# Masks from GpSimd, the up-projection weights in halves, and a new order of the instructions in an attention and maxout kernel

## The chip, the cores and the metric

The kernel runs on one core of a Trainium2 chip. A core has five engines that run side by side, each with its own queue of instructions in a fixed order, and that wait for each other only by semaphores: TensorE (PE, matmuls and transposes; its weight loads are listed as PEld), VectorE (DVE), ScalarE (ACT), GpSimd (POOL) and SyncE (SP), which here only issues DMAs. DMAs move data between the main memory (HBM) and the on-chip buffer (SBUF); matmuls write into eight banks of PSUM, from which DVE or ACT copy. The metric is the device time of one execution in microseconds (us), smaller is better.

## What is computed

Four batches of attention with 8 heads, 768 positions and 64 elements per head, then a feed-forward layer over all 3,072 tokens.

```python
scores = scale * np.matmul(q, k.transpose(0, 1, 3, 2))
stream_keep = causal & (is_sink | in_win)
mask = np.where(retr[0, :, 0, 0, None, None], full_mask, stream_mask)
scores = np.where(mask[None, :, :, :], scores, -1000000000.0)
scores = scores - np.max(scores, axis=-1, keepdims=True)
a = np.exp(scores)
a = a / (np.sum(a, axis=-1, keepdims=True) + 1e-09)
attn = np.matmul(a, v)
x = np.ascontiguousarray(attn_out.transpose(0, 2, 1, 3)).reshape(B * S, H * D)
out = np.maximum(x @ w1, x @ w2) @ w_out      # 512 -> 1024 -> 512
```

Three of the eight heads (`is_retrieval`) are causal over all earlier positions; the other five see the first 4 positions (sinks) and a window of 64.

## The kernel before, in words

**Heads and tiles.** The kernel finds at run time which heads are full and sorts the heads (`head_order`, L1483), so that four pairs of heads are worked: full with full, full with streaming, and two pairs of streaming heads (`SLOTS`). Each batch is worked in two halves of 384 queries, written (b, hf). Of the scores only blocks of 128 keys by 128 queries that some mask lets through are computed; the tables `GROUP0` (first halves), `GROUP1` (second halves) and `GROUP_A` (first half of batch 0) put these blocks into score tiles of two PSUM banks each. For streaming heads a "mixed" key block holds the 64 sink positions beside 64 positions of the window (`mix_k`, `mix_v`, tiles `kx`, `vx`).

**Steps of one half.** q, k and v arrive as float32 in a slot of `ld` (three slots, which the two up-projection weights share with the batches). They are cast to bf16 (`cast_qk` into `qb`, `cast_v` into `vb`), q and k are turned by PE (`turn`, L712, into a PSUM bank) and copied out (`unturn`, into `qk`). Score tiles (L893, 64 rows of the array at a time, two heads beside each other) are exponentiated by ACT from PSUM into `at` (L912, six buffers), masked by DVE through a product with 0/1 masks (L931), and multiplied with v (`weighted`, L956), where a column of ones gives the sum. DVE divides (L973, L983) into `x`. `x` is turned by PE in batch 0 (L1086) and by a DMA in the others (L1105). In (0, 0) the masks are added to the scores by matmuls of the identity with rows of the mask table instead (L867). For batch 3, q, k and v are cast by the DMA that loads them (`load_pair`, L558, issued by POOL) and turned by DMA (L583).

**Feed-forward.** max(h1, h2) = relu(h1 - h2) + h2, so the kernel prepares w12 = w1 - w2 (four subtractions on DVE, L1122, a quarter of the columns each) and w2·w_out (`prep_weights`: cast w2 to `w2b`, turn it, L1138, and multiply it by `wob`, the bf16 w_out, L1156). For each half, `forward` does 32 up-projection matmuls (L1177) with relu on ACT or DVE (L1201, L1203), and 12 matmuls per 128 tokens (L1227): four of x with w2·w_out and eight of the relu with w_out. The result goes over `ot` to HBM (L1246).

**What sets the order.** Nothing here is scheduled by the compiler. The program records operations with their costs, dependencies, PSUM claims and ranks (`Op`, `Order`), and `Order.run` (L190) plays them against a model of the engines, the PSUM banks and the DMA rings. In the order in which that play begins them, they are emitted into the engines' queues. For PE it takes the first list in `PE_LISTS` whose next operation is ready for at least a `MARGIN`; for DVE, ACT and POOL, an operation that several could do goes to the one that would be done first, waiting operations in order of `RANK`. While nothing is ready before 38 us of that model, PE gets dummy matmuls on a tile of zeros (L471), which keep its clock up. Parameters such as `RANK`, `MARGIN`, `LOADS`, `RATE`, `STEP` were found by a search over orders.

**Loads.** `LOADS` gives the first loads in order: A and B are q and k of the first and second half of batch 0, Av and Bv their v, w10 to w23 the quarters of w1 and w2, wo0 to wo3 the quarters of w_out. SP issues them (`whole` L513, `piece` L523 for v, `load_up` L608), w_out goes through POOL with a cast (L616). The mask table, 128 x 1,152 in bf16, is a constant in HBM: its first 128 columns (the identity) are loaded from ACT's queue (L1570), the other 1,024 from SP's (L595) behind q and k. From it DVE makes 0/1 masks (`kept`, L646).

**Runs of scores.** `TOGETHER` (L113) names which score tiles are issued as one operation of PE: in pairs for all halves but the first, where they are single.

## Time and profile before

| | |
|---|---|
| time, median of 3 runs | 184.38 us (184.33 to 184.59) |
| the profiled execution's own time | 183.78 us |
| its span, first to last instruction | 180.9 us |
| granted TensorE clock | 0.999 |
| PE busy | 171.1 us (95%) |
| ACT busy | 131.7 us (73%) |
| DVE busy | 96.7 us (53%) |
| POOL busy | 42.8 us (24%) |
| DMA | 32.67 MB, mean 181 GB/s |

The profile is one execution, taken by the hardware. Line numbers (L1177) are those of the kernel before; a helper that records operations of many kinds has one line for all (L480 is every copy on ACT, L482 every copy on DVE or POOL). The rows are of these kinds: busy time of each engine in a stretch (us of the span, with the number of instructions, the granted clock PEclk as a share, the busy share of the DMA engines and GB/s); the chain that ended last (start, length, what, xN instructions merged); the timeline (start, length, engine, line, operation, out<-in, shape, count, and in brackets how long the engine had been idle and what ended that); groups by line. A busy PE is not PE at its peak, because the ends of pipelined matmuls are modelled.

### The profile page before, as it was taken

What the parts mean: (1) busy time and instruction counts of PE and PEld (TensorE: products, weight loads), DVE (VectorE), ACT (ScalarE), POOL (GpSimd) and SP (SyncE); (2) the same over time, 40 slices, a digit from 0 to 9 for tenths busy, and PEclk for the clock granted to TensorE, in tenths of its full rate; (3) what the DMA queues carried; (4) which work ended last, traced back from release to release, by engine and by line L of the source; (5) the groups of instructions that cost most, each with busy time, mean ns of one, the idle gap of its engine ahead of it and who ended that gap; (6) DMA issues with size and microseconds to landing.
All of it is one profiled execution on the core that took longest, in us unless ns stands there. A gap on an engine that the chain in (4) does not pass through costs nothing.

```text
span 180.9 us, 4911 instructions
## 1 busy us (share of the span) xinstructions
PE 171.1 (95%) x1816; PEld 106.2 (59%) x1836; DVE 96.7 (53%) x283; ACT 131.7 (73%) x287; POOL 42.8 (24%) x77
## 2 busy tenths in 40 slices
PE   7899599989999999999999999999999999999992
PEld 7767486466747656565545565565466645545561
DVE  3456796599788985576247476656448500000000
ACT  3399695597999999999996984677798524525421
POOL 0000710100609488799671000000000000000000
PEclk9999999999999999999999999999999999999999
DMA  5999999999999999999999999160151052012013
GB/s 139 323 253 336 343 224 242 344 298 278 254 297 273 323 293 284 150 250 217 147 102 136 236 173 200 66 145 0 62 145 62 0 145 116 11 58 116 0 60 125
DMA packets 74929, 32.67 MB, mean 181 GB/s; under 512 B 54162, under 2 KB 71826, under 8 KB 74898
## 3 DMA queue, kind: packets, MB, share of 16 engines
q1 hardware_dynamic: 54704, 28.71, 64.9%
q0 software_dynamic: 19904, 3.41, 26.4%
q8 instruction: 16, 0.26, 0.6%
q10 hardware_dynamic: 290, 0.16, 0.3%
q14 instruction: 15, 0.12, 0.2%
HBM read 25.46 MB, written 6.29 MB: 176 GB/s over the span
## 4 chain that ended last, share of the span: by engine, by line
PE 73%; SPq 11%; DMA 6%; ACT 3%; DVE 3%; issue 2%; DVEq 0%; ACTq 0%
PE ps L1227 32%; PE ps L1177 24%; PE ps L893 7%; PE ps L956 7%; DMA ld<-in_v_dram 6%; SPq L523 5%; SPq L608 4%; PE ps L712 3%; ACT at L912 2%; SPq L513 2%; DVE w L1122 1%; SPq L595 1%; ACT qk L480 1%; DVE vx L482 1%; DVE vb L482 0%
## 5 line engine op out<-in xcount | busy, mean ns | idle before, releaser
L912 ACT ACTIVATE at<-ps 128x512 bf16<-128x512 f32 (+2 forms) x134 | 64.9, 595 | 3.5 <-PE ps L893 1.9
L1177 PE MATMUL ps<-xt,w 128*128 128x384 bf16 x256 | 46.0, 326 | 0.9 <-DVE w L1122 0.6
L1227 PE MATMUL ps<-wob,g 128*128 128x512 bf16 (+1 forms) x192 | 45.3, 370 | 0.4
L1177 PEld LDWEIGHTS <-w 128*128 128x128 bf16 x256 | 23.5, 98 | 15.9 <-issue 0.9
L1201 ACT ACTIVATE g<-ps 128x384 bf16<-128x384 f32 x56 | 27.5, 503 | 7.0 <-PE ps L1177 6.5
L931 DVE TENSOR_TENSOR at<-at,tab 128x1024 bf16<-128x1024 bf16 (+5 forms) x49 | 25.5, 537 | 12.7 <-ACT at L912 12.4
L1227 PEld LDWEIGHTS <-g 128*128 128x128 bf16 x200 | 18.1, 98 | 17.6 <-issue 0.2
L480 ACT COPY ot<-ps 128x512 f32<-128x512 f32 (+1 forms) x20 | 11.4, 572 | 22.8 <-PE ps L1227 22.7
L1227 PE MATMUL ps<-w2o,xt 128*128 128x512 bf16 (+1 forms) x91 | 24.2, 370 | 0.6
L956 PEld LDWEIGHTS <-at 128*128 128x128 bf16 x477 | 19.8, 97 | 7.3 <-issue 0.2
L983 DVE TENSOR_TENSOR x<-ps,rez 128x192 f32 x64 | 22.8, 356 | 1.8 <-DVE x L983 0.2
L956 PE MATMUL ps<-vb,at 128*128 128x65 bf16 x387 | 21.6, 193 | 0.0
L893 PE MATMUL ps<-qk 64*128 64x128 bf16 (+1 forms) x322 | 20.1, 230 | 0.3
L482 POOL CAST qb<-ld 128x384 bf16 x23 | 11.9, 551 | 35.5 <-DMA ld<-in_k_dram 35.5
L893 PEld LDWEIGHTS <-qk 64*128 64x128 bf16 x322 | 11.9, 94 | 11.2 <-issue 8.2
L1227 PEld LDWEIGHTS <-xt 128*128 128x128 bf16 x100 | 9.2, 98 | 8.8 <-issue 0.2
L480 ACT COPY qk<-ps 128x768 bf16<-128x768 bf16 x17 | 12.9, 817 | 0.6 <-PE ps L712 0.6
L471 PE MATMUL ps<-warmer 128*128 128x128 bf16 x147 | 12.1, 250 | 1.1 <-POOL warmer L1564 1.1
L712 PE MATMUL ps<-tab,qb 128*128 128x128 bf16 x144 | 10.4, 219 | 2.9 <-POOL qb L482 2.1
L480 ACT CAST qb<-ld 128x384 bf16 (+1 forms) x23 | 8.8, 452 | 5.1 <-DMA ld<-in_k_dram 3.1
L471 PEld LDWEIGHTS <-warmer 128*128 128x128 bf16 x147 | 10.9, 115 | 1.4 <-POOL warmer L1564 1.1
L712 PEld LDWEIGHTS <-qb 128*128 128x128 bf16 x144 | 8.4, 98 | 4.0 <-POOL qb L482 2.7
(62 smaller groups left out, 146.1 us busy)
## 6 DMA issues: line engine op xcount, KB each, us to landing
out_dram<-ot SPq DMA_DIRECT2D x23, 256.0 KB, 2.3
ld<-in_q_dram SPq DMA_DIRECT2D x6, 768.0 KB, 6.8
ld<-in_k_dram SPq DMA_DIRECT2D x6, 768.0 KB, 7.7
ld<-in_v_dram SPq DMA_DIRECT2D x18, 256.0 KB, 6.7
ld<-in_moe_w_dram SPq DMA_DIRECT2D x8, 512.0 KB, 8.2
wob<-in_moe_w_out_dram POOLq DMA_DIRECT2D x4, 256.0 KB, 8.5
ld<-in_q_dram POOLq DMA_DIRECT2D x8, 96.0 KB, 7.0
ld<-in_k_dram POOLq DMA_DIRECT2D x8, 96.0 KB, 7.2
```

The source lines that it names most:

```text
L471: nc.tensor.matmul(banks[e][:, 0:128], lhsT=warm, rhs=warm, start=True, stop=True)
L480: nc.scalar.copy(out=out, in_=in_)
L482: eng[e].tensor_copy(out=out, in_=in_)
L712: nc.tensor.transpose(to[:, i], qbs[:, T["qb", n, hf] % NQB, t, i].rearrange("p h d -> p (h d)"), ident)
L893: nc.tensor.matmul(to.rearrange("p (i c) -> p i c", c=128), lhsT=lhsT, rhs=q_of(n, i, m)[rows], start=bk not in under, stop=True, skip_gro ...
L912: nc.scalar.activation(out=at[:, bk, 0:w], in_=bank(("ps", b, hf, t), part=bk)[:, 0:w], func=ACT.Exp, scale=scale,)
L931: eng[e].tensor_tensor(out=at, in0=at, in1=tbl, op=ALU.mult)
L956: nc.tensor.matmul(po[:, hh, i - NT * hf, :], lhsT=ats[:, T["at", b, hf, t] % NAT, bk, e * 128:(e + 1) * 128], rhs=rhs, start=first, stop= ...
L983: nc.vector.tensor_tensor(out=xs[:, (2 * b + hf) % NX, :, bass.ds(heads[2 * p + hh], 1), :], in0=po[:, hh, :, 0:D].unsqueeze(2), in1=z[:, ...
L1177: nc.tensor.matmul(bank(key)[:, 0:HALF], lhsT=w[:, kc, fc * 128:(fc + 1) * 128], rhs=xts[:, (2 * b + hf) % NXT, :, kc, :], start=(kc == 0) ...
L1201: nc.scalar.activation(out=g, in_=ph, func=ACT.Relu)
L1227: nc.tensor.matmul(bank(key)[:, cols], lhsT=lhsT, rhs=(w2o if kind == "x" else wob)[:, c, cols], start=(e == 0), stop=(e == len(steps) - 1),)
```

## The change

Before and after compute the same. Six things differ.

1. **Masks.** The constant in HBM and its two loads are gone. DVE zeroes the table and POOL fills it: `affine_select` once for the identity and seven times in `mask_table` for the additive masks, and two copies. The order's model takes the masks as given at 6.5 us.
2. **w1 and w2 in two parts of columns.** Each is loaded in two pieces of 512 columns instead of four of 256. The four subtractions and casts stay quarters, each waiting for the half that it lies in.
3. **q and k of batch 0 apart.** `SPLIT` now holds (0, 1) beside (0, 0). q and k of these halves are cast by separate operations (those of (0, 0) were before), and new for both: turned by separate PE operations (`TQ` for q, `TK` for k) into banks of their own, and copied out by separate copies.
4. **Scores in runs.** `TOGETHER` is gone, every score tile is an operation of its own. The order prefers a further score tile when the last PE operation was one, starts a run only when `S_RUN` tiles are ready with banks free (`run_of_scores`), and its model counts a price for entering and leaving a run.
5. **Loads of w_out** are held back by POOL: each but the first copies one element of an earlier load's place (`landed`) before it issues, and so waits for that load. The model limits outstanding descriptors on POOL's ring too.
6. **The order searched anew**: all ranks, margins and rates, with ranks of their own for batch 0 (`FRONT`, `rank_of`), eight `at` buffers instead of six, and a new `LOADS`. The buffer of the final test on the sums (`ok`) now lies in a load slot.

The general path for other head patterns (`tile_any_heads`), which doesn't run here, uses three score matmuls of 256 columns instead of two of 384.

```diff
--- before
+++ after
...
-TOGETHER = (
-    [[0, 1], [2, 3], [4, 5], [6]], [[0, 1], [2, 3], [4, 5], [6, 7], [8, 9]],
-    [[0], [1], [2], [3], [4], [5]],
-)
...
+    def run_of_scores(self, first, t):
+
+        mine = self.lists["S"][first:]
+        mine = [o for o in mine if o.tag[1:3] == mine[0].tag[1:3]]
+        n = 1 if self.stuck or mine[0].tag[1:3] == (0, 0) else min(S_RUN, len(mine))
+        if len(mine) - n == 1 and not self.stuck:
+            n += S_REST
+        if any(o.left or o.ready > t + 1e-9 for o in mine[:n]):
+            return False
+        return sum(e is None for e in self.banks) >= 2 * n
...
-                    for n in names:
+                    for n in ("S", *names) if last == "S" else names:
...
+                        if n == "S" and last != "S" and not self.run_of_scores(at[n], t):
+                            continue
...
+                        extra = ENTER_S if n == "S" and last != "S" else LEAVE_S if last == "S" and n != "S" else 0.0
+                        last = n
...
+MASKS_MADE = 6.5
...
-NAT = 6
+NAT = 8
...
-PE_LISTS = ('TX', 'W', 'S', 'TQ', 'P', 'H', 'P2', 'F')
-PLACES = (0, 1, 2, 0, 1, 2, 0, 1, 2, 0, 1, 2)
+PE_LISTS = ('TX', 'W', 'S', 'TK', 'TQ', 'P', 'H', 'P2', 'F')
...
-LOADS = (
-    'A', 'Av', 'B', 'w23', 'wo0', 'wo1', 'wo2', 'w20', 'wo3', 'w21', 'w11', 'w10', 'w12', 'w22',
-    'w13', 'Bv',
-)
-BIAS = {'DVE': 1, 'ACT': 0}
+LOADS = ('A', 'wo0', 'B', 'w20', 'w10', 'Av', 'wo1', 'wo2', 'w11', 'wo3', 'w21', 'Bv')
+BIAS = {'DVE': 0, 'ACT': 0}
...
-PACE = 0
+PACE = 1
...
-SPLIT = ((0, 0),)
+RING = {'SP': 4224, 'POOL': 6200, 'ACT': 4224}
+SPLIT = ((0, 0), (0, 1))
...
+S_RUN = 2
+S_REST = 1
+ENTER_S = 0.1
+LEAVE_S = 0.11
...
-MARGIN = {'W': 2.0, 'S': 0.8, 'F': 2.0, 'TQ': 0.8}
-X_MARGIN = 1.5
+MARGIN = {'W': 1.2, 'S': 0.3, 'F': 0.3, 'TQ': 1.2}
+X_MARGIN = 0.8
...
+FRONT = (
+    {'mix_k': -14.4, 'mask': -3.2, 'unturn': 13.5, 'exp': 11.7, 'vcast': 31.8, 'cast': -27.9,
+    'norm': -5.0}, {'vcast': 9.0, 'unturn': -0.2, 'exp': 16.7, 'mask': 0.7, 'norm': -5.5,
+    'mix_k': 13.8, 'cast': -1.4},
+)
+FRONT_STEP = (22.5, 5.2)
+UNTURN_BIAS = ({'ACT': 1.0}, {})
+SHARED = 0.89
+UP_PARTS = 2
...
+    def rank_of(kind, b, hf, at=0):
+        if b:
+            return RANK[kind]
+        return RANK[kind] + FRONT[hf].get(kind, 0.0) + FRONT_STEP[hf] * at
...
-    def load_table(lo, hi):
-        return dma(0.262, lambda _: nc.sync.dma_start(
-            out=tab[:, lo:hi], in_=table_dram.ap()[:, lo:hi]
-        ), rate=0.4, parts=128, grain=85.0)
...
-        n = d_ff // 4
+        n = d_ff // UP_PARTS
...
+        return dma(
+            2.097 / UP_PARTS, emit, old=staged_old[name], rate=RATE["w"] if UP_PARTS == 4 else RATE["w half"],
+            parts=512, grain=180.0 / UP_PARTS,
+        )
...
+            for o in behind:
+                nc.gpsimd.tensor_copy(out=landed, in_=place_of[o])
...
+    bias_in.append(order.given(MASKS_MADE))
...
+                for lo, hi in ((0, 1), (1, 2)) if (b, hf) in SPLIT else ((0, 2),):
+                    key, m = ("pt", n, hf, lo), hi - lo
+                    tq = pe(
+                        "TK" if lo else "TQ", mm(*[128] * (m * NT)), turn(n, hf, lo, hi),
+                        cs[lo::2] if m == 1 else cs, claims=[(key, 1)],
+                    )
+                    last_turn[n, hf].append(tq)
+                    un = op(
+                        {"DVE": 0.08 + (0.41 if (b, hf) in LONG else 0.2) * m, "ACT": 0.065 + 0.325 * m},
+                        unturn(n, hf, lo, hi), [tq, *old_s],
+                        frees=[key], tag=f"unturn{b}.{hf}.{p}", rank=rank_of("unturn", b, hf, p),
+                        bias=None if b else UNTURN_BIAS[hf],
+                    )
+                    turned[n, hf].append(un)
...
-        for together in TOGETHER[2 if (b, hf) == (0, 0) else hf]:
+        for t in range(len(group)):
...
+            s = pe("S", cost, scores(b, hf, t), deps, claims=[(("ps", b, hf, t), 2)], tag=("S", b, hf, t))
...
+                [w1_in[c * UP_PARTS // 4], w2_in[c * UP_PARTS // 4]], tag=f"sub{c}", rank=RANK["sub"], port=("POOL",),
...
-    ok = keep.tile([128, rez.shape[1]], F32, name="ok")
+    ok = lds[:, 1, 0, 0, 0:rez.shape[1]]
...
+def mask_table(nc, bias, n_sink, window):
+
+    at = lambda i, n=1: bias[:, 128 * i:128 * (i + n)]
+
+    def put(i, n, base, by_key, by_query, fill=-1e30):
+        nc.gpsimd.affine_select(
+            out=at(i, n).rearrange("p (n c) -> p n c", c=128), in_=at(i, n).rearrange("p (n c) -> p n c", c=128),
+            pattern=[[0, n], [by_query, 128]], compare_op=ALU.is_ge, fill=fill, base=base,
+            channel_multiplier=by_key,
+        )
+    put(7, 1, 0, -1, 1)
+    put(0, 1, n_sink - 1, -1, 0)
+    put(1, 2, window - 129, 1, -1)
+    put(2, 1, -n_sink, 1, 0, 0.0)
+    put(3, 3, window - 1, 1, -1)
+    put(3, 1, -n_sink, 1, 0, 0.0)
+    put(3, 3, 0, -1, 1)
+    nc.gpsimd.tensor_copy(out=at(6)[0:64], in_=at(0)[0:64])
+    nc.gpsimd.tensor_copy(out=at(6)[64:128], in_=at(1)[64:128])
...
-    kept = np.concatenate([sinks, near, sinks | near, band0, band, band, mixed, causal], axis=1)
-    table = np.concatenate(
-        [np.eye(128), np.where(kept, 0.0, -1e30)], axis=1
-    ).astype(ml_dtypes.bfloat16)
-    table_dram = nc.inline_tensor(table, name="mask_table")
...
+        nc.vector.memset(tab[:, 0:1152], 0.0)
+        nc.gpsimd.affine_select(
+            out=tab[:, 0:128], in_=tab[:, 0:128], pattern=[[1, 128]], compare_op=ALU.not_equal, fill=1.0,
+            base=0, channel_multiplier=-1,
+        )
+        mask_table(nc, tab[:, 128:1152], n_sink, window)
...
-        nc.scalar.dma_start(out=tab[:, 0:128], in_=table_dram.ap()[:, 0:128])
...
```

More of the change, by code (lines that the diff above doesn't have):

```diff
@@ L243, in serve @@
                     break
-                total = sum(r[0][1].grain for r in busy)
+                total = sum(r[0][1].grain for r in busy) * (SHARED if len(busy) > 1 and all(r[0][1].grain < 20 for r in busy) else 1.0)
                 first = min(r[0][0] * total / r[0][1].grain for r in busy)
@@ L258, in serve @@
                 served[1] += 1
-                total = sum(r[0][1].grain for r in busy)
+                total = sum(r[0][1].grain for r in busy) * (SHARED if len(busy) > 1 and all(r[0][1].grain < 20 for r in busy) else 1.0)
                 push(t + min(r[0][0] * total / r[0][1].grain for r in busy) + 1e-6, served[1])
@@ L368 @@
 RANK = {
-    'cast': 3.05, 'vcast': 13.85, 'unturn': 4.05, 'mix_k': -0.7, 'mix_v': -14.35, 'exp': 4.1,
-    'mask': -5.1, 'norm': -4.75, 'take_x': -8.75, 'turn': 8.65, 'w2b': 9.4, 'sub': -4.6, 'w2t':
-    -8.95, 'wob': -4.45, 'w2o': -10.4, 'relu': -0.25, 'load': 10.7, 'out': -0.6, 'h2': 7.85,
-    'table': -2.75, 'vload': -2.25,
+    'cast': 8.0, 'vcast': 10.45, 'unturn': 6.55, 'mix_k': -4.7, 'mix_v': -16.7, 'exp': 3.7,
+    'mask': -7.6, 'norm': -7.5, 'take_x': -1.15, 'turn': 0.05, 'w2b': 5.75, 'sub': -6.2, 'w2t':
+    -4.8, 'wob': -3.6, 'w2o': -3.6, 'relu': 3.45, 'load': 6.6, 'out': -5.4, 'h2': 7.9, 'table':
+    -3.65, 'vload': -0.55,
 }
@@ L494, in dma @@
         return o
-    number, freed, loads, later = [0], {}, {}, []
+    number, freed, loads, later, asked = [0], {}, {}, [], []
     def slot():
@@ new lines, in attend @@
+            exps[t] = list(both_)
+            for part in group[t][1] if (b, hf) not in BIASED else ():
+                cols = 128 * part[1] * part[3]
+                exps[t].append(op(
+                    {"DVE": 0.07 + cols / 1920}, mask(b, hf, t, part),
+                    both_[part[0]:part[0] + part[1]] + table_in, tag=f"mask{b}.{hf}.{t}", rank=rank_of("mask", b, hf, t), port=("DVE",),
+                ))
+            done[t] = mine
+            for p in range(HP):
+                if used(b, hf, t, p):
+                    last_s.setdefault(b * HP + p, []).append(s)
@@ L1267, in tile_three_full_heads @@
             if b and b not in CAST_BY_DMA:
-                load_half(b, hf)
+                load_half(b, hf, [t for t in range(3) if (b, hf, t) not in loads])
             order.shift = STEP * (2 * b + hf)
```

220 lines of the change are left out of this document (100 added, 120 removed).

## The prediction

> **What bounds the kernel now.** I read the page first, then busy time by stretch, then the chain that ended last, then the timeline of the first 40 us. Two rows of the page:
>
> ```profile
> span 180.9 us, 4911 instructions
> PE 171.1 (95%) x1816; PEld 106.2 (59%) x1836; DVE 96.7 (53%) x283; ACT 131.7 (73%) x287; POOL 42.8 (24%) x77
> ```
>
> TensorE (PE) is busy 95% of the span, but some of that is warm-up (dummy) matmuls. Busy time by stretch, whole kernel first, then the dummies (L471) alone:
>
> ```profile
> core 0: us, PE busy (x) PEld busy (x) DVE busy (x) ACT busy (x) POOL busy (x), PEclk, DMA share, GB/s
> 0.00:7.66 7.66, 6.54 (x74) 6.55 (x75) 2.62 (x22) 2.60 (x6) 0.83 (x6) 1.00 0.76 218
> 7.66:38.90 31.24, 27.40 (x410) 19.25 (x410) 22.16 (x62) 24.35 (x51) 4.98 (x8) 1.00 1.15 295
> 44.67:143.47 98.80, 97.57 (x1111) 58.87 (x1122) 64.43 (x181) 86.34 (x194) 36.97 (x63) 1.00 1.12 176
> 143.47:177.44 33.97, 33.78 (x182) 17.80 (x183) 1.83 (x9) 13.39 (x26) 0.00 (x0) 1.00 0.22 75
> ```
> ```profile
> 7.66:38.90 31.24, 5.60 (x77) 4.39 (x74) 1.00 1.15 295
> ```
>
> Until 7.66 PE does only dummies; until 38.90, 27.40 us of work of which 5.60 are dummies; from 38.90 on it is full. So the end is the time of the first up-projection matmul (L1177, at 38.90) plus the real work left then. The chain says what sets 38.90:
>
> ```profile
> 21.97 11.74 DMA ld<-in_v_dram
> ...
> 36.57 2.28 DVE w L1122 x2
> 38.90 3.42 PE ps L1177 x20
> ```
> ```profile
> 141.92 0.24 PE ps L956 x8
> ...
> 151.24 1.95 PE ps L1177 x12
> ...
> 169.88 7.54 PE ps L1227 x46
> 177.44 0.37 ACT ot L480
> ```
>
> The initial loads hold the front: the last v piece of batch 0's second half lands at 33.71, VectorE works through casts, mixed values and the subtractions that make w12, and PE's long run starts. It ends at 177.44, so what follows the first up-projection takes 138.54 us. The rest of the span, 3.46 us (last copy and store), is not touched.
>
> **The sum, against the profiled execution** (span 180.9, its own time 183.78; the median of the runs is 184.38, 0.60 more).
>
> *Loads.* Table and w_up as they stand:
>
> ```profile
> L595 SPq DMA_DIRECT2D tab<-mask_table x1: 1636/1636/1636, 2.0 to 2.0; - x1
> ```
> ```profile
> L608 SPq DMA_DIRECT2D ld<-in_moe_w_dram x8: 507/1582/3574, 11.2 to 32.5; - x8
> DMA to landing us min/median/max: 7.1/8.2/10.2
> ```
> ```profile
> 9.00:12.00 3.00, 2.85 (x47) 2.15 (x47) 1.80 (x7) 3.00 (x8) 0.00 (x0) 1.00 1.34 222
> 17.00:21.00 4.00, 1.95 (x43) 1.82 (x41) 2.95 (x10) 2.18 (x6) 1.95 (x3) 1.00 1.11 350
> ```
>
> The last weight piece is issued at 32.5 and lands 7.1 later, at 39.6. The 256 KB table leaves the stream: 0.262 MB at 350 GB/s, 0.75 us. The eight w pieces (1 KB rows, 350 GB/s while alone) become four with 2 KB rows. No row shows 2 KB rows alone. The ends are: no quicker (0), and 10% quicker, a tenth of 4.19 MB at 350 GB/s, 1.2 us; a loss has no row for it, since longer rows mean fewer packets. I take a third, 0.4, being nearest to the 350 row. The four wob loads stay beside others: the first now beside batch 0's q and k, the rest beside w2's second half and v. New order on SP's queue: q, k of both halves, w2 first half, v, w2 second half, v, w1 in two halves. Last landing 39.6 - 0.75 - 0.4 = 38.4 (37.6 to 38.9).
>
> The Trainium skill, "DMA: Bandwidth & Descriptors", section "Where 436 GB/s comes from", puts the HBM limit of a core at about 358 GB/s, which row 350 all but reaches; by that the larger rows buy nothing and the sum is 0.4 us worse, 183.3. No run here shows 2 KB rows alone.
>
> *First up-projection.* w1's first half lands half a transfer (1.05 MB at 350 GB/s, 3.0) before the last: 35.4. One subtraction is half of the 2.28 row, 1.14, so w12's first quarter stands at 36.6. PE must also be through. Behind w2's second half it has 16 transposes, 26 of the w2·w_out matmuls, 34 score matmuls in three runs, 12 transposes of x and 30 weighted sums. Prices:
>
> ```profile
> 28.11 1.06 PE L1138 MATMUL ps<-tab,w2b 128*128 128x128 bf16 x16
> 30.46 5.79 PE L1156 MATMUL ps<-wob,w2t 128*128 128x512 bf16 x25
> ```
> ```profile
> 22.34 0.84 PE L1086 MATMUL ps<-tab,x 128*128 128x128 bf16 x12
> ```
> ```profile
> 113.39 0.44 PE ps L893 x12
> 113.83 0.35 PE ps L956 x8
> ...
> 115.04 0.24 PE ps L956 x8
> ```
>
> 1.06 + 26 x 0.23 + 34 x 0.037 + 3 x 0.11 + 0.84 + 30 x 0.03 = 10.4. Behind that half of w2 there are still 0.79 MB of v, 2.1 of w1 and most of 1.57 of wob to land, 4.2 MB or 12 us at 350 GB/s, so it lands near 26.4; with a cast (0.7) PE is through by 37.5, less what it does while it waits. Between 36.6 and 37.5 I take 36.9: 2.0 earlier than 38.90 (ends 35.8 and 38.3).
>
> *What is left then.* From the order of the two programs: before the first up-projection there now stand 93 instead of 117 score matmuls and 78 instead of 94 weighted sums, so 24 x 0.037 + 16 x 0.03 = 1.4 us more is left. Dummies behind the first real transposes are 89 instead of 73; they stand where PE waits for loads. If one of these waits ends early they cost their own time, at most the longest row of 23, 1.7 us at 5.60/77 each, off the end that I keep.
>
> *Runs of scores.* The eight weighted sums after a run take 0.35 against 0.24: leaving a run costs 0.11. Entering has no row of its own, 0 to as much again. Behind the first up-projection the runs go from 25 to 22: 3 x 0.11 to 0.22, I take 0.5.
>
> *Sum:* -2.0 + 1.4 - 0.5 = -1.1 on PE's chain. With the ends of each term that is -2.4 (35.8, 0.66 for the runs) to +0.5 (38.3, 0.33). In the steady part the chain leaves PE and goes through ACT's exps at two places:
>
> ```profile
> 69.99 1.57 ACT at L912 x3
> 71.56 0.70 ACT qk L480
> ...
> 128.07 1.59 ACT at L912 x3
> ```
>
> The stretch 44.67 to 143.47 has 98.80 - 97.57 = 1.2 us without a matmul. With eight buffers of `at` in place of six an exp waits less often for the weighted sums that read its buffer; I take a third of the 1.2 as gained, 0.4 (ends: all of it, and the stall of rival 2). Forecast: -1.5, so 183.78 becomes 182.3 and the median 184.38 becomes 182.9.
>
> *Masks by GpSimd.* No select is in the trace. Nearest rows:
>
> ```profile
> 0.85 0.20 POOL L1564 MEMSET warmer<- 128x128 bf16 x1 [0.29 <-POOLq L1607]
> 4.61 0.42 POOL L464 MEMSET vb<- 128x384 bf16 x1 [3.55 <-DVE warm L1571]
> 5.94 1.11 ACT L480 CAST qb<-ld 128x192 bf16 x4 [1.94 <-DMA ld<-in_q_dram]
> 8.43 0.87 DVE L482 CAST qb<-ld 128x192 bf16 x3 [1.35 <-DMA ld<-in_k_dram]
> 9.21 0.63 DVE L646 TENSOR_SCALAR tab<-tab 128x128 bf16<-128x128 bf16 x4
> 18.97 1.34 ACT L480 CAST qb<-ld 128x384 bf16 x3 [1.24 <-DMA ld<-in_k_dram]
> 19.05 1.24 POOL L482 CAST qb<-ld 128x384 bf16 x2 [14.02 <-DMA ld<-in_k_dram]
> 20.24 3.16 POOL L616 DMA_DIRECT2D wob<-in_moe_w_out_dram  x4
> ```
>
> Eight selects (five of 128 columns, one of 256, two of 384) and two half copies. By the memsets: 5 x 0.20 + 0.31 + 2 x 0.42 + 2 x 0.20 = 2.6. By the casts (0.62 for 384, taken also for the short ones as the upper end): 6.2. They begin when DVE has zeroed the table (first instruction, some 0.6 us from 0.92): 1.6, so masks stand between 4.2 and 7.8. On DVE's queue the four table operations (L646, 0.63) now wait for them ahead of every cast; the casts of q may start at 5.94, those of k at 8.43. ACT takes six of eight of q's casts and four of k's, and PE needs k, so on DVE even 7.8 + 0.63 ends with k's landing: cost 0. POOL itself then still has the memset of vb (0.42), the first wob issue (3.16/4 = 0.79) and one cast each of q and k (0.6 each at most) to do, the last at 10.2 against 9.3 for DVE's three casts of k: 0.9 late at the upper end, which ACT's idle time in the front covers (rival 1); I take 0. Both masks and identity no longer come by DMA; on ACT's queue that frees one issue ahead of its first casts, which wait for q anyway.
>
> *Without a price on the path:* batch 0's q and k turned apart. In the second half sixteen casts of 192 columns (1.11/4 = 0.28) stand for eight of 384 (1.34/3 = 0.45), 0.9 us more; in both halves sixteen copies out of PSUM stand for eight twice as large, and by the same fixed part of a cast (0.28 - 0.17 = 0.11) that is another 0.9; together 2 us on DVE and ACT, which idle 9.1 and 6.9 us in 7.66 to 38.90. PE may turn q when q has landed, before k: it gives PE work earlier, but PE waits later for the same last load, so 0.
>
> ```profile
> L482 DVE CAST qb<-ld 128x384 bf16 x3 | 1.4, 501 | 0.9 <-DMA ld<-in_k_dram 0.9
> ```
>
> DVE takes 14 more of the full-size casts (POOL 18 fewer, some of them now small): 14 x 0.50 = 7 us, most of it in the stretch where DVE is busy 64.43 of 98.80. POOL's loads of batch 3 follow its casts, so they start no later. Three one-element copies on POOL hold the last three wob issues back until first-half v has landed; behind them on POOL stand only v's second-half casts, which land later still, and who waits for wob are the w2·w_out matmuls counted above. w1's two halves wait on SP until the casts have freed their slot, with batch 1's loads behind them; by the same rates first-half v lands near 23 and is cast within 2 us, while w1's turn on SP comes only behind second-half v. The rez test writes into a load slot that was read long before: 0.
>
> **The rivals.** (1) Masks late, slower. Behind DVE's table operations stand all its casts, and behind POOL's selects its own casts and wob. ACT idles 31.24 - 24.35 = 6.9 us in the front, of which I count half as slack; masks later than 8 + 3.5 = 11.5 cost one for one, and from 13.0 the kernel is slower than before. With masks at 15 it gives 182.9 + 3.5 = 186.4; at three times the cast rows (18.6 + 1.6 = 20.2), 191.6. For it: nothing like a select has been timed. Against: POOL's first cast of the kernel (19.05) took 0.62, no sign of a first-use stall.
> The Trainium skill, "GPSIMD Engine Reference", section "2.1 Instruction dispatch", says that the first call of a freshly loaded kernel pays some 6 us without a visible instruction. On the selects that would put the masks at 10.2 to 13.8, so 182.9 to 185.2, for which I keep a third of this rival's chance; the trace of before has no such pause ahead of POOL's memsets or casts.
>
> (2) The exps become the bound, slower. 20 more up-projection matmuls (3.25 us by 1.95 for 12) now stand behind the last weighted sum (141.92 in the chain), so attention must end 3.25 us earlier relative to PE's end, while ACT is busy 86.34 of 98.80 in that stretch: its 12.5 us of idle shrink to about 8.5. If these pauses can't shrink at all, PE stalls 3.9: 186.8; half of it 184.9. It decides from 1.5.
>
> (3) The loads end no earlier (wob before k's turn, shared rows): first up-projection at 38.3, then -0.6 + 1.4 - 0.5 - 0.4 = -0.1: 184.3.
>
> (4) The new order also removes PE's idle time of the front, up-projection at 35.8: -1.1 more, 181.8.
>
> **How the numbers follow.** Differences within 0.2%, 0.37 us, count as none. Chances: forecast 0.42 (its own range 182.0 to 183.9), (4) 0.18, (3) 0.13, (2) 0.18, (1) 0.09. Faster: 0.42 + 0.18, and 0.06 from the near halves of (1) to (3): 0.66. Same: 0.07, most of (3). Slower: 0.27. The range leaves out the far halves of (1) and (2) and the far tail of (4): 181.0 to 185.8.
>
> **What would show it.** Right: first up-projection near 36.9, the last w1 half landed near 38.4, masks done before 8, some 36 runs of scores become 31, the end of PE near 176. Wrong: DVE's first cast waiting for GpSimd past 9; a first up-projection at 38 or later; PE waits on exps between 45 and 140 that add up to over 1.5 us.

## The result and the profile after

The changed kernel takes **182.72 us** (median of 8 runs, 182.32 to 183.20) against 184.36 (8 runs, 183.59 to 185.78) for the kernel before; the ratio is **0.9902, 95% interval 0.9875 to 0.9928**. The forecast was 182.9 with faster as the likeliest. The number came out right, but not along the way that it was worked out: the forecast has the gain in PE's work inside the span, and it lies outside.

The head of the page of the changed kernel:

```profile
span 181.3 us, 4989 instructions
PE 174.2 (96%) x1838; PEld 108.7 (60%) x1838; DVE 101.7 (56%) x303; ACT 132.1 (73%) x294; POOL 40.1 (22%) x80
```

This execution took 182.93 us. Its span is 0.4 us *longer* than that of before (180.9, of 183.78). What fell is the time that lies outside the span, from 2.9 to 1.6 us. It does so in every execution: before, the time is 2.6 to 3.3 us above the span (median 2.93), after it is 1.58 to 1.65 above it, and the spans themselves have nearly the same median (181.2 and 181.1).

Busy time by stretch, cut at 7.80 (PE's first real transposes stand at 6.84, a few later ones at 7.80), at the first up-projection, at the end of attention and at PE's last matmul; behind it the dummies alone in the second stretch:

```profile
core 0: us, PE busy (x) PEld busy (x) DVE busy (x) ACT busy (x) POOL busy (x), PEclk, DMA share, GB/s
0.00:7.80 7.80, 6.59 (x72) 6.31 (x73) 4.14 (x26) 3.10 (x8) 5.36 (x18) 1.00 0.74 210
7.80:38.10 30.30, 28.41 (x374) 19.75 (x374) 22.11 (x61) 21.45 (x50) 5.40 (x15) 0.94 1.11 297
38.10:143.47 105.37, 104.72 (x1207) 64.54 (x1208) 75.05 (x215) 93.35 (x210) 29.32 (x47) 1.00 1.09 182
143.47:177.97 34.50, 34.50 (x189) 18.12 (x187) 0.44 (x3) 13.85 (x27) 0.00 (x0) 1.00 0.18 66
```
```profile
7.80:38.10 30.30, 8.12 (x88) 6.34 (x87) 0.94 1.11 297
```

The front, until the first up-projection, is fuller (28.41 of 30.30 us busy), but 8.12 us of it are dummies, 2.5 us more than before. Part of that is a clock of 0.50 from 16.30 to 19.71, where 18 of these dummies take 2.75 us. The chain that ended last:

```profile
3.84 11.87 DMA ld<-in_k_dram
...
25.36 11.44 DMA ld<-in_moe_w_dram
36.82 1.24 DVE w L1164
38.10 2.77 PE ps L1219 x16
...
170.17 7.81 PE ps L1269 x48
```

It goes as the forecast had it: first half of w1, one subtraction, first up-projection. But the half lands at 36.80 and not at 35.4, and the first up-projection stands at 38.10 and not at 36.9. PE's last matmul ends at 177.97, 0.56 *later* than before (177.41).

### The profile page after: what moved, and what is told of

Read it like the earlier page. It is cut to its first block, busy times and chain, and to the rows that moved or that the text cites. A ratio compares the mean times of both kernels' runs of the same rounds, so it can differ in the third digit from the quotient of the medians.

```text
span 181.3 us, 4989 instructions
## 1 busy us (share of the span) xinstructions
PE 174.2 (96%) x1838; PEld 108.7 (60%) x1838; DVE 101.7 (56%) x303; ACT 132.1 (73%) x294; POOL 40.1 (22%) x80
## 3 DMA queue, kind: packets, MB, share of 16 engines
q0 software_dynamic: 19904, 3.41, 25.7%
## 4 chain that ended last, share of the span: by engine, by line
PE 70%; DMA 13%; DVE 7%; ACT 4%; issue 2%; SPq 2%; DVEq 0%; POOL 0%; ACTq 0%; POOLq 0%
PE ps L1269 31%; PE ps L1219 20%; DMA ld<-in_k_dram 7%; PE ps L945 7%; PE ps L1008 6%; DMA ld<-in_moe_w_dram 6%; PE ps L756 2%; ACT at L964 2%; DVE x L1035 2%; SPq L551 2%; PE ps L503 1%; ACT vb L512 1%; DVE at L983 1%; DVE qb L514 1%; PE ps L1198 1%
## 5 line engine op out<-in xcount | busy, mean ns | idle before, releaser
L964 ACT ACTIVATE at<-ps 128x512 bf16<-128x512 f32 (+2 forms) x134 | 66.1, 590 | 5.2 <-PE ps L945 4.5
L1269 PE MATMUL ps<-wob,g 128*128 128x512 bf16 (+1 forms) x200 | 47.6, 371 | 0.0
L983 DVE TENSOR_TENSOR at<-at,tab 128x1024 bf16<-128x1024 bf16 (+5 forms) x49 | 24.5, 514 | 14.9 <-ACT at L964 14.5
L503 PE MATMUL ps<-warmer 128*128 128x128 bf16 x149 | 14.3, 258 | 1.4 <-POOL warmer L1613 1.2
L756 PE MATMUL ps<-tab,qb 128*128 128x128 bf16 x144 | 12.6, 227 | 1.7 <-POOL qb L514 1.2
L514 POOL CAST vb<-ld 128x192 bf16 x21 | 8.1, 424 | 26.2 <-DMA ld<-in_v_dram 26.2
L503 PEld LDWEIGHTS <-warmer 128*128 128x128 bf16 x149 | 12.2, 119 | 1.5 <-POOL warmer L1613 1.2
L514 DVE COPY qk<-ps 128x384 bf16<-128x384 bf16 (+1 forms) x17 | 10.2, 642 | 3.9 <-PE ps L756 3.9
L512 ACT CAST qb<-ld 128x192 bf16 (+1 forms) x26 | 9.5, 425 | 3.8 <-DMA ld<-in_k_dram 2.0
L756 PEld LDWEIGHTS <-qb 128*128 128x128 bf16 x144 | 9.6, 101 | 3.8 <-POOL qb L514 1.4
```

The source lines that it names most:

```text
L503: nc.tensor.matmul(banks[e][:, 0:128], lhsT=warm, rhs=warm, start=True, stop=True)
L512: nc.scalar.copy(out=out, in_=in_)
L514: eng[e].tensor_copy(out=out, in_=in_)
L756: nc.tensor.transpose(to[:, i], qbs[:, T["qb", n, hf] % NQB, t, i].rearrange("p h d -> p (h d)"), ident)
L964: nc.scalar.activation(out=at[:, bk, 0:w], in_=bank(("ps", b, hf, t), part=bk)[:, 0:w], func=ACT.Exp, scale=scale,)
L983: eng[e].tensor_tensor(out=at, in0=at, in1=tbl, op=ALU.mult)
```

## The experiments

Two questions: where the 1.3 us outside the span come from, and what the parts of the change do inside it. Theory A was that the time outside goes with the mask table in HBM; theory B, that the 2.9 us belonged to one execution and the gain lies inside; C and D are stated with their runs. In this table "order kept" means that PE's order of work is that of the kernel that was edited; "tail" is the time from the end of PE's last matmul to the end of the profiled execution's time. First up-projection and tail are of the profiled execution; span, time outside it and time are medians. Each ratio is to executions of before taken beside that run; over all of these before has a median of 184.19, and its span and time outside are of these, while its 184.36 is that of the result.

| kernel | order kept | first up-projection | tail | span | outside the span | time | ratio to before |
|---|---|---|---|---|---|---|---|
| before | | 38.90 | 6.37 | 181.2 | 2.93 | 184.36 | |
| after | | 38.10 | 4.96 | 181.1 | 1.60 | 182.72 | 0.9902 |
| b_masks | no | 37.60 | 5.73 | 181.3 | 2.11 | 183.36 | 0.9975 (0.9949 to 1.0000) |
| a_table | no | 37.84 | 5.01 | 184.0 | 1.69 | 185.71 | 1.0082 (1.0053 to 1.0110) |
| b_fallback | yes | 38.48 | 5.60 | 181.4 | 1.90 | 183.25 | 0.9959 (0.9932 to 0.9986) |
| a_fallback | yes | 37.14 | 7.72 | 184.1 | 1.60 | 185.67 | 1.0091 (1.0061 to 1.0121) |
| a_nofall | yes | 37.56 | 5.03 | 180.4 | 1.80 | 182.20 | 0.9892 (0.9864 to 0.9919) |
| a_nohold | yes | 41.93 | 4.87 | 185.9 | 1.65 | 187.52 | 1.0178 (1.0151 to 1.0206) |
| a_nowo | yes | 36.86 | 4.91 | 180.45 | 1.60 | 182.07 | 0.9883 (0.9849 to 0.9917) |
| a_1kb | yes | 39.38 | 5.13 | 181.85 | 1.66 | 183.50 | 0.9959 (0.9932 to 0.9986) |
| a_tabdma | yes | 37.63 | 5.45 | 182.3 | 1.73 | 184.03 | 1.0000 (0.9966 to 1.0035) |
| a_four | no | 36.19 | 5.12 | 187.75 | 1.65 | 189.41 | 1.0306 (1.0244 to 1.0368) |
| a_masks2 | yes | 38.72 | 4.89 | 183.25 | 1.63 | 184.87 | 1.0039 (1.0019 to 1.0059) |
| a_noruns | no | 40.62 | 5.22 | 186.9 | 1.68 | 188.57 | 1.0232 (1.0199 to 1.0264) |

### Masks alone, and the table put back

b_masks is the kernel before with the masks made by GpSimd; a_table is the changed kernel with the table loaded again. In both the order was planned anew.

```diff
 # b_masks (a_table: the other way round)
-    table_dram = nc.inline_tensor(table, name="mask_table")
...
-        nc.scalar.dma_start(out=tab[:, 0:128], in_=table_dram.ap()[:, 0:128])
...
-                bias_in.append(load_table(128, 1152))
...
+        nc.vector.memset(tab[:, 0:1152], 0.0)
+        nc.gpsimd.affine_select(
+            out=tab[:, 0:128], in_=tab[:, 0:128], pattern=[[1, 128]], compare_op=ALU.not_equal, fill=1.0,
+            base=0, channel_multiplier=-1,
+        )
+        mask_table(nc, tab[:, 128:1152], n_sink, window)
```

> The kernel before with one part of the change: masks and identity made by DVE and GpSimd, no mask table in HBM, no load of it; its order follows from its own parameters. Theory A (the gain is in time outside the span, and goes with the table): the changed kernel's time minus span is 1.6 us in every run against 2.88 in the one profile of before, so this kernel shows 1.6 as well and comes to about 183.0, 1.3 under before, whatever its span does. Theory B (2.88 was that one execution's; the gain is in the order inside the span): time minus span stays as in the other runs of before, and the time moves by at most the 0.75 us of stream that the table took, 183.6 to 184.4.

> The changed kernel with the table back in HBM, loaded from ACT's and SP's queues as before, no mask made by GpSimd; the rest as changed. Theory A: time minus span goes back to 2.9 us and the time to about 184.0 or above, with the span within 0.7 of the changed kernel's. Theory B: time minus span stays at 1.6; the time rises by at most the table's 0.75 us in the load stream, 182.7 to 183.5.

b_masks moves the first up-projection 1.3 us forward and leaves the span where it was; 0.8 us go outside it. a_table has the table and only 1.69 us outside the span. So theory A falls: the time outside doesn't go with the table. Theory B falls too, as the spans of before and after agree. a_table's span is 2.9 us longer though its first up-projection lies where the changed kernel's does; a_tabdma, below, takes the planning out of that.

### The general path behind the end

The list of the change ends with a sentence on `tile_any_heads`, code that lies behind the last instruction and that all engines skip here. In b_fallback the kernel before gets only this part of the change; in a_fallback the changed kernel gets the old form back; in a_nofall the path isn't there.

```diff
 # b_fallback (a_fallback: the other way round)
-                ps = ps_s.tile([128, 2, 512], F32, tag="s", name="any_ps")
+                ps = ps_s.tile([128, 1024], F32, tag="s", name="any_ps")
...
-                for e in range(2):
-                    cols = slice(e * S // 2, (e + 1) * S // 2)
+                for e in range(3):
+                    cols = slice(e * S // 3, (e + 1) * S // 3)
...
 # a_nofall
-    with tc.If(right < 1):
-        tile_any_heads(tc, *anyhow)
```

> The kernel before with one part of the change alone: the general path for other head patterns, which lies behind the end of the program and doesn't run here, has three score matmuls of 256 columns instead of two of 384. Nothing that runs is touched, so the span stays at 181.1. Theory C: the time outside the span (2.9 us before, 1.6 after) goes with the code that the engines skip at the end. Then it falls from 2.9 to 1.6, and the time from 184.3 to 183.0. Theory D: it goes with something in the code that runs (its length on an engine, the place of its end). Then it stays at 2.9 and the time at 184.3.

> The changed kernel with the general path of before (two score matmuls of 384 columns); all that runs is the changed kernel's. Span 181.1 by both theories. Theory C: time outside the span 1.6 -> 2.9, time 184.0. Theory D: it stays at 1.6, time 182.7.

> The changed kernel without the general path that lies behind it (left out: the computation for other head patterns, which these inputs don't take). All that runs is the changed kernel's, and there is no code left to skip at the end. In a_fallback only PE's instructions of the general path differ from the changed kernel, and the span grew by 3.0 us, all of it between PE's last matmul and PE's drain; so the skip costs by where PE's code stands. Theory: every place costs something, the tail (from the last matmul's end to the end of the time: 4.9 us after, 6.3 before, 7.7 a_fallback) falls below 4.9, to 3.5 to 4.5, and the time to 181.3 to 182.3. Rival: the changed kernel's place already costs nothing, tail 4.9, time 182.7.

Theory C holds in kind, and not in its numbers. Before gains 0.94 us (184.19 to 183.25) from code that doesn't run, all of it outside the span (2.93 to 1.90; the span itself is 0.2 longer). The changed kernel loses 2.95 us with the old form, all of it *inside* the span. Where it sits is seen in SP's waits at the end of the program, on PE's queue first of after, then of a_fallback:

```profile
SPq L1675 <- PEq L1675: 0.7, 2, 0.5
```
```profile
SPq L1675 <- PEq L1675: 3.6, 2, 3.0
```

and in the instructions of the closing line (the last two numbers are the starts of the first and last of them), again after and a_fallback:

```profile
L1675 SPq DRAIN  x3: 7/7/13, 180.3 to 180.7; - x3
...
L1675 PEldq DRAIN  x2: 8/8/8, 180.3 to 180.7; - x2
```
```profile
L1675 SPq DRAIN  x3: 7/7/13, 179.6 to 182.8; - x3
...
L1675 PEldq DRAIN  x2: 8/8/8, 182.5 to 182.9; - x2
```

In a_fallback PE's matmuls end at 177.28 and SP is through at 179.6, but PE reaches its drain only at 182.5, and everybody waits for it; after, the two come together at 180.3. The two programs differ only behind the skip, in a piece that stands there 192 times, with three score matmuls and three DVE operations or with two of each (the expectation of a_nofall names PE's instructions alone; DVE stands at its own branch at 151.4 already). The branch over the path takes PE as long in both, after and then a_fallback:

```profile
L1638 PEldq COMPARE_BRANCH  x1: 3593/3593/3593, 176.5 to 176.5; - x1
```
```profile
L1638 PEldq COMPARE_BRANCH  x1: 3613/3613/3613, 175.8 to 175.8; - x1
```

It begins while PE's last matmuls still run, so most of it is hidden behind them and the last store. After, PE reaches its drain 0.2 us behind the branch; in a_fallback one semaphore follows at 179.43 and then nothing for 3.05 us. In that gap one fetch of 16,384 bytes on the instruction queue q8 runs, from 180.13 to 181.18; after, the like of it starts at 180.79, when PE has passed its drain. DMA queues from 176 us on, after and then a_nofall:

```profile
q1 hardware_dynamic: 288, 0.39, 12.0%
q10 hardware_dynamic: 144, 0.13, 4.2%
q8 instruction: 2, 0.03, 1.4%
q14 instruction: 1, 0.01, 0.3%
```
```profile
q1 hardware_dynamic: 288, 0.39, 11.7%
q10 hardware_dynamic: 144, 0.13, 4.2%
```

With code to skip, instructions are fetched by DMA in the tail; without it, none are. The Trainium skill, "Runtime: NRT & Kernel Launch", section "Instruction fetch mechanics", says that instructions stream in blocks of 16 KiB and that a taken branch to outside the loaded window waits for a fetch of its target. The trace agrees as far as it goes: PE's branch of 3.6 us and its gap of 3.05 us each have one fetch of 16,384 bytes on q8 in them. That it is the place of PE's last instructions relative to such blocks that decides between 0 and 3 us, and what the time of before waits for outside its span, is argued, not shown. The theory stated with a_nofall, that every place costs something, falls: its tail is 5.03, that of after 4.96. So the changed kernel's place costs nothing, that of before costs some 1.4 us (tail 6.37), that of a_fallback 2.8. The same execution order with the code gone is not shown to be better than after (182.20 against 182.72, and the intervals of the ratios overlap).

### The loads

a_nohold drops the three one-element copies that hold the last w_out loads back; a_nowo doesn't load three quarters of w_out; a_1kb issues each w load in two of 1 KB rows; a_tabdma loads the table again; all keep the changed kernel's order. a_four takes four parts of w with an order of loads of its own, planned anew.

```diff
 # a_nohold
-            for o in behind:
-                nc.gpsimd.tensor_copy(out=landed, in_=place_of[o])
 # a_nowo
+            if c:
+                nc.gpsimd.memset(wob[:, 2 * c:2 * c + 2], 0.01)
+                return
 # a_1kb
-            nc.sync.dma_start(
-                out=T[name][:, :, c * n:c * n + n],
+            for lo in (c * n, c * n + n // 2):
+                nc.sync.dma_start(
+                    out=T[name][:, :, lo:lo + n // 2],
...
 # a_tabdma (masks by DVE and GpSimd taken out; identity from ACT's queue)
+                if (b, hf, t) == (0, 0, 1):
+                    nc.sync.dma_start(out=tab[:, 128:1152], in_=table_dram.ap()[:, 128:1152])
 # a_four
-LOADS = ('A', 'wo0', 'B', 'w20', 'w10', 'Av', 'wo1', 'wo2', 'w11', 'wo3', 'w21', 'Bv')
+LOADS = ('A', 'wo0', 'B', 'w20', 'w21', 'w10', 'w11', 'Av', 'wo1', 'wo2', 'w12', 'w13', 'wo3', 'w22', 'w23', 'Bv')
-UP_PARTS = 2
+UP_PARTS = 4
```

> The changed kernel without the three one-element copies on POOL that hold the last three w_out loads back; these loads are then issued from 7 us on, beside q and k, not from 20.5. Theory (the bytes are the same, the stream has gaps at 18 to 21 and runs at some 200 GB/s from 24 to 30): the loads land earlier, last w1 38.0, first up-projection 37.2, time 181.8 to 182.4. Rival: w_out takes its share from q and k, their casts come later, and PE, which works in a fixed order, starts real work later: last k of the second half 18 instead of 15.7, first up-projection 38 to 40, time 183.5 to 185.

> The changed kernel with three quarters of w_out not loaded: POOL fills their places with a constant instead (left out: w_out's last 768 rows, so the output isn't the reference's). 1.57 MB less to load. The prediction's working (the last loads set the first up-projection, and the end follows it): 1.57 MB at 350 GB/s is 4.5 us, the last w1 load lands at 35.0, the first up-projection then waits for PE's chain only, 35.5 to 36.5, span 178.7 to 179.7, time 180.4 to 181.4. Rival: w1 comes no earlier, since SP issues it only when the slot of the first half has been cast; landing 38 or later, span 181.1, time 182.7. Second rival: the first up-projection comes earlier, but PE only waits elsewhere afterwards: up-projection 36, time 182.7.

> The changed kernel in its own order, each w load of 512 columns issued as two of 256 (1 KB rows) one behind the other. Theory (from the trace of after: 2 KB rows moved at some 383 GB/s, 1 KB rows of before at 350): 2.1 MB of w1 take 6.0 us instead of 5.5 and w2's two halves 0.25 each, so the last w1 load lands 0.5 to 1.0 later (40.0 to 40.5), the first up-projection stands at 38.6 to 39.1, time 183.2 to 183.7. Rival, by a limit of HBM that longer rows can't lift: nothing changes, last landing 39.5, time 182.7. Second rival: the loads move but the end doesn't, since PE has other work; landing 40.3, time 182.7.

> The changed kernel with its order of instructions kept as planned, but the masks loaded from HBM again (identity from ACT's queue, 256 KB from SP's behind the first k) in place of memset, selects and copies. a_table, where the order was planned anew as well, had a span 2.9 us longer with the first up-projection at the same place. Theory: that came from the new order, and the table costs what the prediction gave it: 0.262 MB at 350 GB/s, 0.75 us later last w1 landing (40.3), first up-projection at 38.8, span 181.9, time 183.4. Rival: the loading itself disturbs the steady part, span 184.0 as in a_table, time 185.7. Third: the loads don't set the end, span 181.1, time 182.7. Time outside the span 1.6 to 1.7 in each, as a_table had.

> The changed kernel with w1 and w2 loaded in four parts of columns again (1 KB rows). If the 2 KB rows run at some 385 GB/s and the 1 KB rows at 350, the last weight lands 1.1 us later and the time is 0.5 to 1.2 us over the changed kernel's, 183.2 to 183.9. If the rows' length doesn't matter, within 0.3 us of it.

**a_nohold**, 4.8 us slower than after, is the largest effect with the order kept, by another way than its rival named. PE's longest wait, and the piece of the chain before it:

```profile
PE ps L1178 <- DVE w2b L514: 2.9, 1, 2.9
```
```profile
18.03 10.89 DMA ld<-in_moe_w_dram
```

q and k land where they did (the casts of k end PE's wait after 1.0 us, 1.2 after), but w_out now lies ahead of w2's second half, which lands at 28.92 instead of 25.23; PE has nothing to do, its clock is 0.50 from 29.95 to 33.37, and the first up-projection slides to 41.93. The prediction described the hold and gave it no price.

**a_nowo**: w1's halves land at 32.31 and 35.97 (after: 36.80 and 39.54), the first up-projection comes only 1.24 us earlier, since PE's fixed order is by then the limit, and the time falls by 0.65, which isn't clear of noise. The first half of w1 has landed 4.5 us before it is used. So loads that are 1.57 MB lighter are worth less than 1 us, where the prediction's working gives 1.3 to 2.3: second on the critical path, right behind the loads, is PE's own list of the front.

**a_1kb** is 0.8 us slower than after, as its theory had it. But its profiled execution (184.50, 1.0 above its median) shows another way there: the last w1 load lands at 41.23, later than the 40.5 of the theory, and PE's longest wait is for w2's last quarter, which lands at 28.12 behind pieces of v:

```profile
PE ps L1181 <- ACT w2b L512: 2.9, 1, 2.9
```

That 2 KB rows move faster by themselves is seen in stretches in which nearly all that is loaded is w, before (1 KB rows) and after:

```profile
34.00:37.00 3.00, 2.95 (x41) 1.82 (x41) 2.88 (x10) 2.95 (x8) 0.40 (x2) 1.00 1.06 339
```
```profile
32.00:36.00 4.00, 4.00 (x34) 1.95 (x34) 2.51 (x7) 3.88 (x11) 0.92 (x3) 1.00 1.06 386
18.00:19.00 1.00, 1.00 (x12) 1.00 (x10) 0.95 (x5) 0.76 (x3) 0.00 (x0) 0.50 0.75 132
20.00:21.00 1.00, 1.00 (x13) 0.37 (x14) 0.57 (x4) 0.46 (x1) 0.68 (x2) 1.00 0.90 142
```

The other two rows are holes in the stream of after, while v arrives in rows of 256 bytes and SP's next issue has yet to go out.

**a_tabdma** is 1.3 us slower than after, between its theory (0.7) and its rival (3.0), with spans from 180.9 to 183.5; the profiled execution lies at the low end (181.2) and doesn't show what lengthens the others. What it shows is that 1.7 of the 3.0 us by which a_table lies above the changed kernel came from planning anew. **a_four** has its first up-projection early (36.19) and ends late: its order of loads hangs the last w_out load on a piece of w, POOL waits for that until 36.22, and PE waits later. It says nothing on the size of the rows.

### Masks later, and no runs

a_masks2 makes the masks twice, one after the other; a_noruns takes the preference for further score tiles and the hold-back of a run out of the order.

```diff
 # a_masks2
-        mask_table(nc, tab[:, 128:1152], n_sink, window)
+        for _ in range(2):
+            mask_table(nc, tab[:, 128:1152], n_sink, window)
 # a_noruns
-                    for n in ("S", *names) if last == "S" else names:
+                    for n in names:
...
-                        if n == "S" and last != "S" and not self.run_of_scores(at[n], t):
-                            continue
```

> The changed kernel with the seven selects and two copies made twice, so that the masks stand about 3.3 us later, at 8.6, and POOL's first cast of k at 10.3 instead of 7.05. The prediction's working: nothing up to 11.5, one for one beyond: span 181.1, time 182.7. Rival: the front has no such slack, since PE goes through its dummies and real work in a fixed order, and what comes late at 7.8 stays late: first up-projection 3 us later (41.1), span 184.1, time 185.7.

> The changed kernel, but the order neither prefers a score tile behind a score tile nor holds a run back until two tiles are ready: 46 runs of scores in place of 27 (34 in place of 22 behind the first up-projection). If a run costs 0.2 us of PE, 2.4 us more behind the first up-projection: 184.5 to 185.5. If it costs 0.1, 183.5 to 184.3. If other PE waits cover it, no difference to the changed kernel, 182.7.

In a_masks2 the masks stand at 8.6, where the prediction still saw no cost up to 11.5. It costs 2.15 us of time. PE's waits:

```profile
PE ps L756 <- ACT qb L512: 2.1, 1, 2.1
...
PE ps L756 <- POOL qb L514: 0.6, 1, 0.6
```

PE's first transposes come as early as after (6.98 and 6.84). Those that stand at 7.45 after come at 9.67, those at 7.80 at 10.82, and with PE's clock at 0.50 from 9.75 to 13.16 those at 9.02 come at 13.14. By the transposes that wait for the last k (16.28 after, 19.10 here) 2.8 us are left, and at the first up-projection 0.6 in this execution, one of the fastest of its runs. The working (no cost up to 11.5) is wrong; the rival is nearer, though the cost is not its full 3.

a_noruns has 46 runs of scores instead of 27 (bias matmuls counted in), 12 more of them behind the first up-projection, and is 5.85 us slower, where at most 2.8 were expected: 2.5 until the first up-projection, the rest behind it. A run costs 0.19 us by the distances of PE's starts (entering 312 ns where two down-projections lie 216 apart, leaving 148 where two scores lie 56 apart), so 19 runs are 3.6; the remaining 2.2 are waits of an order that no longer fits, such as 1.9 us for `x` ahead of the transposes of w2.

## Why the prediction came out right

It has 183.78 - 1.5 for the profiled execution; 182.93 came. By medians it has -1.5 and -1.64 came, of which -0.1 is inside the span. By its terms, for the profiled pair:

| term | forecast | measured |
|---|---|---|
| first up-projection | -2.0 | -0.80 |
| what is left then | +0.5 (1.4 - 0.5 - 0.4) | +1.36 |
| behind PE's last matmul | 0 | -1.41 |
| sum | -1.5 | -0.85 |

The two errors inside the span (+1.2 and +0.9) are undone for the most part by the one behind it (-1.4). That the number came out right is luck: PE's last matmul, forecast near 176, ends at 177.5 on average in the two profiled executions with the order of before and at 177.6 in the three with all running code changed. With the general path of before, everything else changed, the ratio is 1.0091 and the forecast would have been wrong in sign.

- **"The rest of the span is not touched", and nothing for what lies around it**: the step that failed most. Nothing in the trace of before shows it as a variable, but its pieces were there: a tail of 6.37 us of which the last copy (0.37) and store (1.8 from issue to landing) explain 2.2. PE's branch over the path that isn't run was in that trace too, with 3.66 us.
- **First up-projection at 36.9**: mis-sized. Three profiled executions of the same running code (after, a_fallback, a_nofall) have it at 38.10, 37.14 and 37.56, two of before's (before, b_fallback) at 38.90 and 38.48: 1.1 us earlier, not 2.0. The one of the three that kept its clock throughout, a_fallback, has the earliest. The 10% for 2 KB rows, taken as an upper end, was real (386 against 339 to 350 GB/s), so rival value 183.3 falls. That value rested on the limit of 358 GB/s of the Trainium skill's "DMA: Bandwidth & Descriptors", section "Where 436 GB/s comes from"; the trace goes above it. The Trainium skill's "HBM Reference", section "Specifications (TRN2)", calls 358 a core's share, and says that a core streaming alone goes above it, as here. The last w1 load landed at 39.54, 38.61 and 37.53 in the three. No run isolates what ate the gain. In the same stretch stand the holes in the load stream and 2.5 us more of dummies, for which I had at most 1.7 and counted none. 1.1 us of these come with the halved clock: the 92 dummies from PE's first transposes to the first up-projection take 8.67 us after and 7.57 in a_fallback.
- **The end follows the first up-projection**: right. In eight kernels with the changed order it lies between 36.86 and 41.93, and PE ends 139.9 to 141.0 us behind it.
- **What is left then**: over the same executions it rose by 1.1 (138.84 to 139.96), against 0.5. The 0.4 for gaps without a matmul is the term that failed here: the gaps that it counted on were hardly there. Behind the first up-projection before shows 1.39 us of gaps, but 0.84 of them are sixteen holes of 52 to 54 ns where a matmul's record is missing (its weight load is recorded, and the starts around it lie one step of 216 ns too far apart). Of PE's matmuls 20 are missing in the profile of before (x1816 against x1836 weight loads) and none after (x1838), which shows 0.65. So it isn't shown that the gaps shrank, and of the 1.2 us that the prediction read as time without a matmul 0.69 are such holes. Without this term the forecast is +0.9 against the 1.1. A run costs 0.19, inside 0.11 to 0.22, and by scores alone 36 runs became 31, 25 became 22 of them behind the first up-projection, as forecast (with the bias matmuls between scores counted in, 31 became 27). What is left of the difference stays open.
- **Masks between 4.2 and 7.8, cost 0**: right. POOL's first instructions in after:

```profile
1.73 0.29 POOL L1615 TENSOR_SCALAR_AFFINE_SELECT tab<-tab 128x128 bf16<-128x128 bf16 x1 [0.60 <-DVE tab L1614]
1.98 2.70 POOL L1565 TENSOR_SCALAR_AFFINE_SELECT tab<-tab 128x128 bf16<-128x128 bf16 x7
...
4.97 0.32 POOL L1578 COPY tab<-tab 64x128 bf16<-64x128 bf16 x1
```

  They stand at 5.3; POOL waited 0.60 for DVE's zeros and for nothing else, and no pause of some 6 us is seen ahead of the selects. Those 6 us are what the Trainium skill's "GPSIMD Engine Reference", section "2.1 Instruction dispatch", has for a first call. But the cover that I claimed isn't there: half of ACT's idle time is no slack for PE (a_masks2).
- **Rival 2**, exps as the bound: no. With 20 more up-projections behind attention, PE has 0.65 us of gaps in the 105.37 us from the first up-projection to 143.47. **Rival 3**, loads that end no earlier: its mechanism is what happened (39.54 against 39.6 in the profiled pair), but it ended 1.6 us too late, for the tail was not in it.

No version run here that computes all of the kernel's paths is faster than the changed one.

## What to carry to other kernels

Split every time into three: up to the last instruction of the bounding engine, from there to the end of the span, and outside it; code that is skipped moved the last two by 1 to 3 us here, so a small gain or loss says nothing of the work itself until that is taken off, and the length of the skipped code is worth a run of its own. Before counting small gaps of an engine as time to be won, compare its records with those of its weight loads: missing records look like gaps. Test one part of a change with the order of work kept, since planning it anew can cost more than the part (1.7 of 3.0 us for the table). Idle time of an engine in the front is no slack when the bounding engine runs a fixed list with filler in it; only an experiment that delays the thing tells.

## What the runs showed of the hardware

- **The clock fell by half after a wait of 1.2 us, in one kernel and not in another.** PE's row of the timeline of after with its wait for a cast, and busy time and granted clock of PE behind it:

```profile
16.28 0.49 PE L756 MATMUL ps<-tab,qb 128*128 128x128 bf16 x3 [1.21 <-POOL qb L514]
```
```profile
16.00:17.00 1.00, 0.72 (x8) 0.65 1.18 309
17.00:18.00 1.00, 1.00 (x12) 0.50 1.33 230
18.00:19.00 1.00, 1.00 (x12) 0.50 0.75 132
19.00:20.00 1.00, 1.00 (x9) 0.65 0.96 212
```

  It was 0.5 for 3.4 us. a_nofall, with a wait of 1.14 in the same place, lost half of its clock for 3.4 us there too; a_nowo waited 1.22 and kept 1.00, a_fallback 0.61 and kept it. So such a wait may or may not cost the clock. The Trainium skill, "TensorE: Matmul & The Clock Gate", section "What's actually happening", gives windows of 3.4 us that run freely and a clock that is either full or half. Length and level agree. Free windows would explain part of the chance and not all: in windows of 3.41 us laid from each trace's own changes of clock, 1.48 us (a_nofall) and 1.54 us (after) without a matmul cost the clock, and 1.66 us (before, 16.54 to 19.95) and 1.98 us (a_1kb, 27.31 to 30.72) did not.
- **GpSimd's selects** take 0.29 us for 128 columns of bf16, and seven of them with 1,536 columns together 2.70.
- **A kernel's time depends on code that doesn't run**: its new form in place of the old takes 0.94 us off one kernel and 2.95 off another.
